# One transpose for the row of maxima, five transfers to send it, and a schedule in the source for every attention step

## The chip, the cores and the metric

The kernel runs on one core of a Trainium2 chip. The metric is device time in microseconds (us); the median of three runs of the kernel before is 1284.25 (1282.39 to 1284.72). PE is the matmul engine TensorE, PEld its weight loader, DVE is VectorE, ACT ScalarE, POOL GpSimd, and SP the engine that issues the DMA transfers. Each engine runs its own instructions strictly in program order and waits on semaphores for the others.

## What is computed

```python
q_pool = q.reshape(B, H, S // 2, 2, D).mean(axis=3)        # B=8, H=8, S=1152, D=64
scores = (1 / sqrt(D)) * q_pool @ k.transpose(0, 1, 3, 2)
attn = exp(scores - scores.max(-1, keepdims=True))
attn = attn / (attn.sum(-1, keepdims=True) + 1e-9)
x = heads_side_by_side(attn @ v)                           # (8, 576, 512)
theta = x @ w_theta
y = w_tok_r @ (x * cos(theta)) + w_tok_i @ (x * sin(theta))   # over tokens
u = x + y
out = u + maximum(u @ w_ch, 0)
```

## The kernel before

The first part does the attention of 64 heads as 32 pairs of heads, each pair on the 128 partitions as two times 64; the second part, from `theta` on, does eight batches and is not touched.

A pair goes through these steps (lines of the kernel before). **Operands:** q and k are loaded (L246, L274), q is pooled by DVE (L291, tile `qk`), both are turned by DVE in two pieces into PSUM (`pt`, L320 and L322), copied by ACT as `hi` (L348), and DVE makes the rest `lo` (L359). **Maxima:** 12 groups of two matmuls (`pm`, L374) give scores of 128 queries with 384 keys for both heads, and DVE reduces each (`mx`, L381); the last 64 queries of each head are the tail, `px` and `py` (L391, L395), reduced at L396 and L397. DVE joins the partial maxima into one column of nine per partition (`nm`, L401), turns it (`nt`, L403), and SP sends it as a row to `nmr` (L409, L410). **Scores:** 18 tiles (two halves `u` of 288 queries times nine key groups) of eight matmuls each (`pe`, L429); the last two of a tile add the row `nmr`, so a pair's first tile needs the row. ACT takes the exponential into one of 14 buffers `pc` (L432). **Sums and values:** POOL adds seven of a half's nine `pc` into `ss` (L442); PE sums the rest over keys (`pns`, L478) and multiplies all nine with `v` (`pa`, L456), 36 matmuls per half. Row sums go through memory for a reciprocal and come back as `dn` (L495 to L518); DVE scales and turns the result (L527, L532). Beside it the weights of the second part are brought to the wanted form piece by piece (L562 to L669, tiles `raw`, `wf`, `ws`, `pwt`).

All steps of a pair lie on a scale of 18 units a pair. Tables of numbers (`MAX_AT`, `PREP_AT`, `AV_AT`, `PLAN` and others) give each step's place on it, `plan` enters them for 32 pairs, and the list is emitted in the order of places. That is the order on every engine. PSUM is four slots of two banks of 512 floats. Every matmul result, small ones too, takes a whole slot; `bank2` chooses the slot at emission from three running clocks and the constants of `HOLD`. A step that is given a slot waits until the engine that read its last content is done.

Of the kernel before, what the change touches and what calls it, by code (L numbers as in the profile page):

```python
# [18 lines left out]
TAIL = 7  # L19
TAIL_LAST = 4  # L20
QP_ENG = 'vector'
DVE_SS = ()
PC_BUFS = 14
MAX_AT = (-23.312, -20.226, -18.883, -18.536, -17.347, -14.986, -12.74, -10.103, -9.854, -9.265, -8.03, -7.436)
SS_LAG = 5.804
AV_AT = (((11.793, 9),), ((17.363, 4), (18.395, 5)))
PREP_AT = {'t0': -36.588, 'hi0': -36.387, 'px': -18.64, 'lo0': -36.184, 't1': -24.925, 'hi1': -24.615, 'lo1': -24.124, 'tail': -24.631}
NS_AT = 26.57
AV_WORK = 0.49
W_FIRST = (9.45, 9.5, 9.85, 10.5, 12.75, 18.0, 18.6, 19.25, 20.45)  # L30
W_AT = (7.309, 8.637, 10.414, 10.912, 11.46, 12.125, 16.279, 17.785, 29.189, 44.405)
W_LAST = (9.4, 10.2, 11.0, 11.8, 12.6, 13.4, 14.2, 15.0, 15.8, 16.6, 17.4, 18.2, 19.0, 19.8, 20.6, 21.4, 22.2, 23.0, 23.8, 24.6)
W_END = 30
TURN_AT = 8.506
V_AT = -1.0
PRO = ({'load_k': -75.788, 'load_q': -85.873, 'pool_q': -76.236, 't0': -73.01, 'hi0': -64.408, 'lo0': -15.283, 't1': -68.701, 'hi1': -58.549, 'lo1': -53.475, 'tail': -51.925, 'px': -30.196, 'max_nm': -15.377, 'load_max': -12.729}, {'load_k': -49.139, 'load_q': -68.986, 'pool_q': -46.442, 't0': -23.223, 'hi0': -16.979, 'lo0': -10.648, 't1': -20.324, 'hi1': -14.593, 'lo1': -14.517, 'tail': -6.908, 'px': 1.104}, {'t0': 3.186, 'hi0': 3.765, 'lo0': 3.821})
MAX_AT0 = (-52.472, -50.954, -45.116, -43.942, -41.943, -40.966, -38.157, -37.18, -36.005, -27.822, -27.698, -24.494)
MAX_AT1 = (-32.274, -18.203, -18.096, -17.725, -14.587, -13.206, -13.08, -11.704, -10.826, -8.296, -8.18, -7.244)
PLAN = {'load_q': -54.267, 'load_k': -39.846, 'pool_q': -40.262, 'load_max': -3.215, 'load_v': 9.606, 'max_nm': -6.746, 'norm_spread': 33.247, 'norm_load': 35.19, 'norm_recip': 38.931, 'norm_save': 45.467, 'norm_bcast': 48.28, 'norm_out': 54.162, 'norm_turn': 56.676, 'norm_store': 62.099}
MAN = ("PE", "Activation", "DVE", "Pool", "SP")  # L40
BANKS = {}
SLOTS = 4
HOLD = {'e': (19.92, 'a', 7.517), 'pm': (8.214, 'd', 2.971), 'pt': (7.034, 'ad', 2.722), 'px': (4.719, 'd', 21.159), 'py': (6.753, 'd', 17.042), 'pa': (2.703, 'a', 2.941), 'mt': (8.515, 'a', 6.594), 'ns': (4.437, 'a', 5.407), 'pw': (4.651, 'ad', 6.171)}
# [40 lines left out]
SIN_LIM = 3.1415925  # L84


@with_exitstack
def pooled_attention_moe_kernel(
# [56 lines left out]
    clock = {"p": 0.0, "a": 0.0, "d": 0.0}  # L145
    slots = [0.0] * SLOTS

    def bank2(kind, name):
        n = min(range(SLOTS), key=lambda k: slots[k])
        work, engines, after = HOLD[kind]  # L150
        psum["slot"] = n
        clock["p"] = max(clock["p"], slots[n]) + work
        end = max([clock["p"] + 0.3] + [clock[e] for e in engines]) + after
        for e in engines:
            clock[e] = end
        slots[n] = end + 0.1
        return psum["now"][0].tile([P, 2, 512], F32, tag=f"b{n}", name=name, bufs=1)

# [44 lines left out]
    with ExitStack() as p1:  # L203
        psum["now"] = (
            p1.enter_context(tc.tile_pool(name="ps1", bufs=1, space=bass.MemoryType.PSUM)),
            BANKS,
        )
# [15 lines left out]
        nt = nrm.tile([TB, P], F32, name="nt")  # L223
# [5 lines left out]
        state = {}  # L229

        def load_q(i):
            b, hp = divmod(i, NP)
            h0 = 2 * hp
            qn = inp.tile([P, 4 * QT * D], F32, tag="qn", name=f"qn{i}")
            if i == 0:
                qv = qn[0:QP].rearrange("p (h t f d) -> p h t f d", h=2, t=QT, f=2)
# [3 lines left out]
            else:  # L240
                qn = qn[:, 0:S]
                for h in range(2):
                    qv = q[b, h0 + h].rearrange("(n i t) (e s) -> e i t n s", n=3, i=32, e=2)
                    for e in range(2):
                        a = 32 * (2 * h + e)
                        nc.sync.dma_start(  # L246
                            qn[a : a + 32].rearrange("i (t n s) -> i t n s", n=3, s=32), qv[e]
                        )
            state.setdefault(i, {})["qn"] = qn

        def keys(i):
            st = state.setdefault(i, {})
            if "kn" not in st:
                qk = inp.tile([P, QT * P + S], F32, tag="qk", name=f"qk{i}")
                st["qp"] = qk[:, 0 : QT * P if i == 0 else SQ]
                st["kn"] = qk[:, QT * P :] if i == 0 else qk[:, SQ : SQ + S]
                st["q3k"] = qk[:, 0 : SQ + 3 * P]
            return st["kn"]

        def load_k(i):  # L260
            b, hp = divmod(i, NP)
            h0 = 2 * hp
            kn = keys(i)
            for h in range(2):
                if i == 0:
                    nc.sync.dma_start(
                        kn.rearrange("p (t h d) -> p t h d", t=KT, h=2)[:, :, h, :],
                        k[b, h0 + h].rearrange("(p t) d -> p t d", t=KT),
                    )
                    continue  # L270
                kv = k[b, h0 + h].rearrange("(a i t) (e s) -> e i t a s", a=4, t=KT, e=2)
                for e in range(2):
                    a = 32 * (2 * h + e)
                    nc.sync.dma_start(  # L274
                        kn[a : a + 32].rearrange("i (t a s) -> i t a s", t=KT, a=4), kv[e]
                    )

        def pool_q(i):
# [3 lines left out]
            if i == 0:  # L282
                qv = st["qn"][0:QP].rearrange("p (h t f d) -> p h t f d", h=2, t=QT, f=2)
                ov = qp[0:QP].rearrange("p (t h d) -> p t h d", t=QT, h=2)
                for h in range(2):
                    nc.vector.tensor_tensor(
                        ov[:, :, h, :], qv[:, h, :, 0, :], qv[:, h, :, 1, :], ALU.add
                    )
            else:
                qv = st["qn"].rearrange("p (t f c) -> p t f c", t=QT, f=2)  # L290
                getattr(nc, QP_ENG).tensor_tensor(  # L291
# [3 lines left out]
        def load_v(i):  # L295
# [4 lines left out]
            state[i]["vn"] = vn  # L300

        def prep(i):
            st = state[i]
            for n in ("hi", "lo"):
                st[n] = opd.tile([P, SQ + S], F32R, tag=n, name=f"{n}{i}")
            st["nmr"] = nmrs[i % 2]

        K0 = {t: SQ * (t >= 6) + t * P for t in range(KT)}
        Q0 = 6 * P

        def prep_t(i, g):
# [27 lines left out]
        def prep_parts(i, g):  # L339
            st = state[i]  # L340
            c0, w = ((0, 3 * P), (Q0, 5 * QP))[g]
            return st["pt", g][:, :, 0:w], *(
                st[n][:, c0 : c0 + 2 * w].rearrange("p (b c) -> p b c", b=2) for n in ("hi", "lo")
            )

        def prep_hi(i, g):
            src, hi, lo = prep_parts(i, g)
            nc.scalar.copy(hi, src)  # L348

        def prep_tail(i):  # L350
            st = state[i]
            tl = st["tail"] = tails[i % 2]
            c = QP - HT
            for hs in HEADS:
                nc.scalar.copy(tl[hs, hs], st["pt", 1][hs, 1, c : c + HT])

        def prep_lo(i, g):
            src, hi, lo = prep_parts(i, g)
            nc.vector.tensor_tensor(lo, src, hi.bitcast(F32), ALU.subtract)  # L359
            if i == 0:  # L360
                slots[state[i]["slot", g]] = clock["d"] + 2.0

        HEADS = (slice(0, D), slice(D, P))

        def maxpass(i):
            st = state[i]
            hi = st["hi"]
            mx = st["mx"] = sml.tile([P, KT, 3], F32, tag="mx", name=f"mx{i}")
            W = 3 * P
            for j in range(4):  # L370
                for g in range(3):
                    pm = bank2("pm", f"pm{i}_{j}{g}")
                    for h, hs in enumerate(HEADS):
                        nc.tensor.matmul(  # L374
                            pm[:, h, 0:W],
                            hi[hs, Q0 + j * P : Q0 + (j + 1) * P],
                            hi[hs, K0[3 * g] : K0[3 * g] + W],
                            start=True,
                            stop=True,
                        )  # L380
                    nc.vector.tensor_reduce(  # L381
# [722 lines left out]
```

## Time and profile before

| | |
|---|---|
| median of three runs | 1284.25 us |
| profiled execution, first to last instruction | 1283.3 us |
| PE busy | 1239.1 us (97%) |
| DVE busy | 943.8 us (74%) |
| POOL busy | 748.1 us (58%) |
| ACT busy | 672.5 us (52%) |
| first value product of pair 0 | at 47.00 us |
| first token product of the second part | at 851.37 us |

Shares are over the whole span; the two parts have different limits. Matmuls of two heads run side by side and their bars overlap, so durations of single matmuls do not add up; the distance of two starts is what a step takes. A weight load that waits shows as idle time of PEld.

### The profile page before, as it was taken

The page shows a single profiled execution, that of the slowest core. Times are in us where ns is not written, and L with a number is a line of the kernel's source. Part 1 is how long each engine was busy: PE and PEld are TensorE (multiplying, and loading weights), DVE is VectorE, ACT ScalarE, POOL GpSimd, SP SyncE. Part 2 cuts the span into 40 slices and gives each one's busy share as a digit, 9 for nine tenths or more (in the row PEclk, how much of TensorE's full clock was granted, in tenths as well). Part 3 has the DMA queues.
Part 4 walks back from the last instruction along what each step waited for, and adds up shares of the span by engine and source line. Part 5 has one row for each costly group of instructions (what it writes and reads, how often), then busy time and mean ns, then how long its engine had stood idle before and what let it go on. Part 6 is the DMA issues. An engine that isn't in the chain of part 4 may idle for free.

```text
span 1283.3 us, 29416 instructions
## 1 busy us (share of the span) xinstructions
PE 1239.1 (97%) x11633; PEld 1004.3 (78%) x11633; DVE 943.8 (74%) x1373; ACT 672.5 (52%) x1162; POOL 748.1 (58%) x540
## 2 busy tenths in 40 slices
PE   3999999999999999999999999999999999999998
PEld 2777777767777777777777777688999999999997
DVE  6879988888888888988898897565464655637452
ACT  1566566656656665665666565464343443434430
POOL 0498768778786877778787776634323333232320
PEclk7999999999999999999999999999999999999999
DMA  5646555656656466555556542424534525244231
GB/s 92 128 83 135 116 131 111 122 118 149 119 113 133 111 139 131 120 117 130 123 124 123 119 104 60 126 93 98 103 49 84 97 32 108 39 89 97 36 47 37
DMA packets 482235, 131.05 MB, mean 102 GB/s; under 512 B 451745, under 2 KB 452129, under 8 KB 482097
## 3 DMA queue, kind: packets, MB, share of 16 engines
q1 hardware_dynamic: 481920, 128.71, 47.8%
q8 instruction: 91, 1.49, 0.5%
q0 software_dynamic: 176, 0.46, 0.1%
q14 instruction: 48, 0.39, 0.1%
HBM read 97.21 MB, written 30.70 MB: 100 GB/s over the span
## 4 chain that ended last, share of the span: by engine, by line
PE 83%; DVE 8%; issue 3%; DMA 2%; POOL 2%; ACT 1%; SPq 0%; DVEq 0%; POOLq 0%; ACTq 0%
PE pa L456 20%; PE pe L429 19%; PE py L924 17%; PE pr L963 8%; PE pth L836 8%; PE pm L374 6%; DVE mx L381 4%; PE pns L478 3%; POOL ss L442 1%; DVE qk L291 1%; PE px L391 1%; DMA nmr<-nt 1%; DVE wf L599 1%; DVE mx L396 1%; DMA rc<-rd 1%
## 5 line engine op out<-in xcount | busy, mean ns | idle before, releaser
L442 POOL TENSOR_TENSOR ss<-ss,pc 128x576 f32<-128x576 f32 x314 | 463.5, 1476 | 52.5 <-ACT pc L432 32.2
L381 DVE TENSOR_REDUCE mx<-pm 128x2 f32<-128x768 f32 x384 | 357.0, 953 | 80.0 <-PE pm L374 77.9
L432 ACT ACTIVATE pc<-pe 128x576 f32<-128x576 f32 x576 | 349.8, 652 | 75.0 <-PE pe L429 61.7
L456 PE MATMUL pa<-pc,vn 128*64 128x288 f32 x2304 | 300.4, 410 | 0.4 <-ACT pc L432 0.4
L456 PEld LDWEIGHTS pa<-pc,vn 128*64 128x64 f32 x2304 | 156.9, 137 | 108.7 <-issue 5.7
L924 PE MATMUL py<-wtk,Z 128*128 128x288 f32 x1728 | 233.8, 296 | 0.0
L924 PEld LDWEIGHTS py<-wtk,Z 128*128 128x128 f32 x1728 | 232.3, 189 | 1.3
L897 POOL TENSOR_TENSOR Z<-ab,Z 128x512 fp32r<-128x512 f32 x40 | 52.1, 1303 | 258.8 <-ACT Z L893 251.8
L429 PE MATMUL pe<-hi 64*128 64x288 f32 x1152 | 182.0, 311 | 0.3 <-DVE lo L359 0.2
L429 PE MATMUL pe<-nmr,oner 64*128 64x288 f32 x1152 | 171.2, 292 | 0.0
L429 PE MATMUL pe<-lo,hi 64*128 64x288 f32 x1152 | 170.9, 292 | 0.0
L429 PE MATMUL pe<-hi,lo 64*128 64x288 f32 x1152 | 170.7, 292 | 0.0
L442 POOL TENSOR_TENSOR ss<-pc,pc 128x576 f32<-128x576 f32 x64 | 91.9, 1435 | 126.4 <-ACT pc L432 126.0
L374 PE MATMUL pm<-hi 64*128 64x384 f32 x768 | 145.7, 377 | 16.2 <-ACT hi L348 5.8
L429 PEld LDWEIGHTS pe<-hi 64*128 64x128 f32 x1152 | 109.3, 185 | 24.2 <-issue 7.5
L374 PEld LDWEIGHTS pm<-hi 64*128 64x128 f32 x768 | 73.2, 187 | 64.0 <-DVE mx L381 16.5
L348 ACT CAST hi<-pt 128x768 fp32r<-128x768 f32 x64 | 56.3, 879 | 114.2 <-DVE pt L320 105.3
L429 PEld LDWEIGHTS pe<-lo,hi 64*128 64x128 f32 x1152 | 109.9, 186 | 0.0
L429 PEld LDWEIGHTS pe<-hi,lo 64*128 64x128 f32 x1152 | 109.6, 186 | 0.0
L429 PEld LDWEIGHTS pe<-nmr,oner 64*128 64x128 f32 x1152 | 109.1, 185 | 0.0
L963 PEld LDWEIGHTS pr<-us,wch 128*128 128x128 f32 x768 | 104.2, 189 | 1.6
L963 PE MATMUL pr<-us,wch 128*128 128x288 f32 x768 | 105.2, 296 | 0.0
(101 smaller groups left out, 1426.8 us busy)
## 6 DMA issues: line engine op xcount, KB each, us to landing
vn<-in_v_dram SPq DMA_DIRECT2D x32, 576.0 KB
qn<-in_q_dram SPq DMA_DIRECT2D x124, 144.0 KB
qk<-in_k_dram SPq DMA_DIRECT2D x124, 144.0 KB
dn<-ro SPq DMA_DIRECT2D x64, 144.0 KB
xd<-xu SPq DMA_DIRECT2D x32, 288.0 KB
xbd<-xb SPq DMA_DIRECT2D x32, 288.0 KB
xT<-xd SPq DMA_DIRECT2D x8, 1152.0 KB
xn<-xbd SPq DMA_DIRECT2D x140, 64.0 KB
```

Of the source, the lines that this page charges most:

```text
L348: nc.scalar.copy(hi, src)
L374: nc.tensor.matmul(pm[:, h, 0:W], hi[hs, Q0 + j * P : Q0 + (j + 1) * P], hi[hs, K0[3 * g] : K0[3 * g] + W], start=True, stop=True,)
L381: nc.vector.tensor_reduce(mx[:, j : j + 5 : 4, g : g + 1], pm[:, :, 0:W], AX.X, ALU.max)
L429: nc.tensor.matmul(pe[:, h, 0:HALF], w[hs], x[hs], start=(n == 0), stop=(n == 3))
L432: nc.scalar.activation(pcs[u, kt], pe[:, :, 0:HALF], AF.Exp, scale=SC)
L442: eng.tensor_tensor(st["ss", u], first, st["pc"][u, kt], ALU.add)
L456: nc.tensor.matmul(pa[hs, 0, 0:HALF], st["vn"][:, h, (kt + 3) % KT, :], st["pc"][u, kt][:, h, :], start=(kt == 0), stop=(kt == KT - 1),)
L478: nc.tensor.matmul(px[a : a + 32, 1, 0:HALF], ones, sets[u][n][:, h, :], start=(n == 0), stop=(n == len(sets[0]) - 1), tile_position=(0, a),)
L836: nc.tensor.matmul(th, xs[c][:, j * P : (j + 1) * P], ws[:, c], start=(n == 0), stop=(n == 11))
L897: engine("zlo", b).tensor_tensor(Z[1], t, Z[0].bitcast(F32), ALU.subtract)
L924: nc.tensor.matmul(st["py", c, u][:, 0:HALF], Z[zi][:, c * P : (c + 1) * P], wtk[wi][:, kw, u * HALF : (u + 1) * HALF], start=(i == 0 and ...
L963: nc.tensor.matmul(pr[u][:, 0:HALF], wch[wi][:, c, e * P : (e + 1) * P], st["us", ui][:, c, u * HALF : (u + 1) * HALF], start=(n == 0), st ...
```

## The change

Two things. First, the row of maxima: `nt` is now 128 x 32, DVE turns `nm` in one instruction, so that the nine rows of each 32 queries stand in four blocks of partitions; five transfers (four for the blocks, one for the tail) put them in place, each for both heads. Second, the tables and `plan` are gone. `operations` lists every step with its engine, the time it keeps the engine, its latency, what it depends on and how it uses PSUM; `schedule` keeps a clock per engine, the PSUM banks and the 14 buffers, and always takes the step that can begin first. In the steady pairs each engine's next step is given by `PLACE` (and one weight step beside it), so the table sets the order there; for the first two pairs and the last it may look eight steps ahead. Value products, row sums and the tail's last piece now take one bank of a slot (`acq` 2, `half`). The arithmetic is the same.

```diff
-        nt = nrm.tile([TB, P], F32, name="nt")
+        nt = nrm.tile([P, TB], F32, name="nt")
...
-            for g in range(0, P, TB):
-                nc.vector.transpose(nt[:, g : g + TB], nm[g : g + TB])
+            nc.vector.transpose(nt, nm)
...
-            for h in range(2):
-                row = nmr[h * D : h * D + 1]
-                nc.sync.dma_start(row[:, 0 : 4 * P], nt[4 * h : 4 * h + 4])
-                nc.sync.dma_start(row[:, 4 * P : SQ], nt[8:9, h * HT : (h + 1) * HT])
+            rows = nmrs[op.i % 2].bitcast(F32).rearrange("(h d) c -> h d c", h=2)[:, 0]
+            g = op.a
+            if g < 4:
+                dst = rows[:, 0 : 4 * P].rearrange("h (c g r) -> h c g r", c=4, g=4)[:, :, g]
+                src = nt[TB * g : TB * g + 8]
+            else:
+                dst = rows[:, 4 * P : SQ].rearrange("h (g r) -> h g r", g=2)
+                src = nt.rearrange("(g c) r -> g c r", g=4)[:, 8]
+            nc.sync.dma_start(dst, src)
...
-AV_AT = (((11.793, 9),), ((17.363, 4), (18.395, 5)))
...
+    "av11": 19.00002, "av12": 19.28072, "av13": 19.82686, "av14": 19.97701, "av15": 20.54731,
...
+        s["nt"] = add(DVE, 0.212, 0.22, "nt", i, "nm", 0.001, [s["nm"]] + back(i, 1, "lm"))
...
+                prev = add(PE, 0.482, 0.642, "av", i, f"av{u}", 0.01 * k, [X[u, k], s["lv"], prev or first], COL64, a=u, b=k, acq=2 * int(k == 0))
...
+    def ahead(e):
+        if e == SP:
+            return 24
+        edge = main[e] and (main[e][0].i < 2 or main[e][0].i >= NPAIRS - 1)
+        return LOOK if edge else 1
...
+        for op in schedule(operations()):
+            steps[op.name](op)
```

How the order moves is shown at two places. The first is PE in the middle of the program, from the tail maxima of one pair to the second value product of the pair before it (`pa_1` before; `b_101` to `b_104` are the four slots afterwards), with the semaphores that a row waits for. Before:

```order
L391 MATMUL px_8297<-hi_7937,tail_120 128x512 [waits DVE_49]
L391 MATMUL px_8297<-hi_7937,tail_120 128x256 x2
L395 MATMUL py_8301<-hi_7937,tail_120 128x128 [waits Activation_49]
L456 MATMUL pa_1_8305<-pc_10_8118,vn_7912 64x288 [waits Activation_49]
L456 MATMUL pa_1_8305<-pc_10_8118,vn_7912 64x288
L456 MATMUL pa_1_8305<-pc_11_8136,vn_7912 64x288 x2
L456 MATMUL pa_1_8305<-pc_12_8152,vn_7912 64x288 x2
L456 MATMUL pa_1_8305<-pc_13_8196,vn_7912 64x288 x2
L374 MATMUL pm_10_8318<-hi_7937 128x384 [waits DVE_49]
```

In the change:

```order
L784 MATMUL b_104<-hi_7162,tail_124 128x512 [waits Activation_49]
L784 MATMUL b_104<-hi_7162,tail_124 128x256 x2
L784 MATMUL b_103<-hi_7162,tail_124 128x128 [waits Activation_49]
L844 MATMUL b_103<-pc_10_7334,vn_6824 64x288 x2
L844 MATMUL b_103<-pc_11_7346,vn_6824 64x288 x2
L844 MATMUL b_103<-pc_12_7353,vn_6824 64x288 x2
L844 MATMUL b_103<-pc_13_7416,vn_6824 64x288 [waits DVE_49]
L844 MATMUL b_103<-pc_13_7416,vn_6824 64x288
L844 MATMUL b_103<-pc_14_7431,vn_6824 64x288 x2
L844 MATMUL b_103<-pc_15_7443,vn_6824 64x288 x2
L844 MATMUL b_103<-pc_16_7455,vn_6824 64x288 x2
```

The value product was left after four of its nine tiles for a pm and a score tile, and is now run through; it stands in the same slot as the tail's last piece, and its fourth tile waits for DVE. The tail's first piece waits for ACT instead of DVE.

The second place is DVE between two pairs, from the last pm reduction of one (`mx<-pm`) to the tail of the next. Before:

```order
L381 TENSOR_REDUCE mx_6289<-pm_32_6607 128x2
L322 STREAM_TRANSPOSE pt_18_6624<-qk_6305 128x2x480
L401 TENSOR_REDUCE nm<-mx_6289 128x9
L403 STREAM_TRANSPOSE nt<-nm 32x32 x4
L359 TENSOR_TENSOR lo_6394<-pt_18_6624,hi_6393 128x960
L381 TENSOR_REDUCE mx_6675<-pm_00_6676 128x2
L291 TENSOR_TENSOR qk_6691<-qn_6402 128x576
L381 TENSOR_REDUCE mx_6675<-pm_01_6725 128x2
L381 TENSOR_REDUCE mx_6675<-pm_02_6757 128x2
L396 TENSOR_REDUCE mx_6675<-px_6763 128x2
```

In the change:

```order
L770 TENSOR_REDUCE mx_6021<-b_103 128x2
L709 STREAM_TRANSPOSE b_102<-qk_5994 128x2x480
L747 TENSOR_TENSOR lo_6116<-b_102,hi_6115 128x960
L770 TENSOR_REDUCE mx_6358<-b_101 128x2
L793 TENSOR_REDUCE nm<-mx_6021 128x9
L796 STREAM_TRANSPOSE nt<-nm 128x32
L770 TENSOR_REDUCE mx_6358<-b_102 128x2
L911 TENSOR_TENSOR xu_5661<-xu_5661,dn_6263 128x576
L770 TENSOR_REDUCE mx_6358<-b_102 128x2
L790 TENSOR_REDUCE mx_6358<-b_104 128x2
```

`nm` and `nt` stand two rows later, behind `lo` and the next pair's first reduction; the pooling of q has left the place after that reduction, and the scaling of an older pair (`xu`) stands after the second.

## Rows read from the trace of the kernel before

**Rows 1.** The page's costliest groups: POOL's additions; busy us, mean ns, idle before.
```profile
L442 POOL TENSOR_TENSOR ss<-ss,pc 128x576 f32<-128x576 f32 x314 | 463.5, 1476 | 52.5 <-ACT pc L432 32.2
```
**Rows 2.** Stretches: us, busy us of PE, PEld, DVE, ACT, POOL, granted clock, DMA.
```profile
25.00:50.00 25.00, 17.02 (x150) 13.64 (x152) 23.02 (x34) 12.35 (x22) 11.33 (x8) 0.73 0.47 93
...
400.00:500.00 100.00, 98.49 (x1084) 72.12 (x1080) 88.78 (x121) 60.46 (x107) 79.19 (x57) 1.00 0.59 127
```
**Rows 3.** The chain that ended last, in time: start us, us, what.
```profile
47.00 4.52 PE pa L456 x36
...
121.80 4.52 PE pa L456 x36
...
796.47 4.52 PE pa L456 x36
...
851.37 21.59 PE py L924 x162
```
**Rows 4.** Timeline of PE within one pair: start us, us, what; idle before.
```profile
402.16 0.30 PE L429 MATMUL pe<-hi 64*128 64x288 f32 x2
...
402.69 0.29 PE L429 MATMUL pe<-hi 64*128 64x288 f32 x2
...
403.75 0.34 PE L374 MATMUL pm<-hi 64*128 64x384 f32 x2
403.93 0.30 PE L429 MATMUL pe<-hi 64*128 64x288 f32 x2
...
405.00 0.33 PE L374 MATMUL pm<-hi 64*128 64x384 f32 x2
405.94 0.74 PE L391 MATMUL px<-hi,tail 128*128 128x512 f32 x3 [0.61 <-DVE mx L381]
...
406.67 2.16 PE L456 MATMUL pa<-pc,vn 128*64 128x288 f32 x16
408.90 0.44 PE L374 MATMUL pm<-hi 64*128 64x384 f32 x2
409.18 0.31 PE L429 MATMUL pe<-hi 64*128 64x288 f32 x2
...
409.82 2.65 PE L456 MATMUL pa<-pc,vn 128*64 128x288 f32 x20
412.39 0.44 PE L374 MATMUL pm<-hi 64*128 64x384 f32 x2
...
417.79 0.69 PE L478 MATMUL pns<-ss,ones 128*32 128x288 f32 x8
...
419.38 0.44 PE L374 MATMUL pm<-hi 64*128 64x384 f32 x2
```
**Rows 5.** Groups on PEld, 121.8 to 771.7 us (26 pairs): busy, mean ns, idle before.
```profile
L429 PEld LDWEIGHTS pe<-hi 64*128 64x128 f32 x936 | 88.2, 184 | 17.8 <-DVE lo L359 5.3 <-issue 4.8 <-DVE wf L595 1.3
L374 PEld LDWEIGHTS pm<-hi 64*128 64x128 f32 x624 | 58.7, 184 | 39.8 <-DVE mx L381 10.7 <-issue 9.0 <-DVE xu L527 6.1
...
L391 PEld LDWEIGHTS px<-hi,tail 128*128 128x128 f32 x78 | 12.6, 188 | 15.8 <-DVE mx L381 14.2 <-issue 0.6
```
**Rows 6.** Groups on DVE in the same stretch.
```profile
L381 DVE TENSOR_REDUCE mx<-pm 128x2 f32<-128x768 f32 x313 | 291.6, 953 | 64.4 <-PE pm L374 62.7
...
L403 DVE STREAM_TRANSPOSE nt<-nm 32x32 f32<-32x32 f32 x104 | 20.8, 200 | 1.9
```
**Rows 7.** Timeline of SP: the row's first and last of four transfers.
```profile
426.91 0.81 SPq L409 DMA_DIRECT2D nmr<-nt  x1
...
429.12 0.52 SPq L410 DMA_DIRECT2D nmr<-nt  x1
```
**Rows 8.** Timeline of PE: the first score tile that uses this row.
```profile
433.79 0.29 PE L429 MATMUL pe<-hi 64*128 64x288 f32 x2
```
**Rows 9.** The chain within 700 to 706 us.
```profile
701.52 2.95 DMA nmr<-nt
```
**Rows 10.** Timeline of PE: the first score tile of the kernel.
```profile
33.13 0.44 PE L429 MATMUL pe<-hi 64*128 64x288 f32 x2
```

More of the change, by code (lines that the diff above doesn't have):

```diff
@@ L84, with __init__ @@
 SIN_LIM = 3.1415925
+class Op:
+    def __init__(self, eng, busy, lat, name, i, a, b, place, off, deps, mode, acq):
+        self.eng, self.busy, self.lat, self.name = eng, busy, lat, name
+        self.i, self.a, self.b, self.place, self.off = i, a, b, place, off
+        self.deps = [d for d in deps if d is not None]
+        self.mode, self.acq, self.owner, self.last, self.ends = mode, acq, None, False, 0
+        self.takes, self.readers, self.reads, self.two = False, 0, [], False
+        self.slot = None
@@ L143, in bank @@
         return pool.tile([P, 512], F32, tag=kind, name=name, bufs=bufs[kind])
[L145 to L157, printed above, removed]
     def segments(j):
@@ L203, in pooled_attention_moe_kernel @@
     with ExitStack() as p1:
[L204 to L207, printed above, removed]
+        ps1 = p1.enter_context(tc.tile_pool(name="ps1", bufs=1, space=bass.MemoryType.PSUM))
+        slots = [ps1.tile([P, 2, 512], F32, name=f"b{n}") for n in range(SLOTS)]
         inp = p1.enter_context(tc.tile_pool(name="inp", bufs=1))
@@ L363, in pooled_attention_moe_kernel @@
[L363 to L381, printed above, removed]
-                        mx[:, j : j + 5 : 4, g : g + 1], pm[:, :, 0:W], AX.X, ALU.max
-                    )
-                    yield
@@ new lines, in prep_lo, with maxima, max_mm @@
+        def prep_lo(op):
+            src, hi, lo = prep_parts(op.i, op.a)
+            nc.vector.tensor_tensor(lo, src, hi.bitcast(F32), ALU.subtract)
+        def maxima(i):
+            st = state[i]
+            if "mx" not in st:
+                st["mx"] = sml.tile([P, KT, 3], F32, tag="mx", name=f"mx{i}")
+            return st["mx"]
+        def max_mm(op):
+            hi, j, g = state[op.i]["hi"], op.a, op.b
+            q = Q0 + j * P
+            pm = slots[op.slot]
+            for h, hs in enumerate(HEADS):
+                nc.tensor.matmul(
+                    pm[:, h, 0:W],
+                    hi[hs, q : q + P],
+                    hi[hs, group(g)],
+                    start=True,
+                    stop=True,
+                )
@@ new lines, in max_red, with half, tail_mm @@
+        def max_red(op):
+            j, g = op.a, op.b
+            nc.vector.tensor_reduce(
+                maxima(op.i)[:, j : j + 5 : 4, g : g + 1], slots[op.slot][:, :, 0:W], AX.X, ALU.max
+            )
+        def half(op):
+            return slots[op.slot // 2][:, op.slot % 2]
+        def tail_mm(op):
+            st = state[op.i]
+            if op.a == 0:
+                parts = [(slots[op.slot][:, n, c : c + w], k) for n, c, k, w in TAIL_KEYS]
+            else:
+                parts = [(half(op)[:, 0:P], Q0 + SQ + 2 * P)]
+            for out, k in parts:
+                nc.tensor.matmul(
+                    out, st["tail"], st["hi"][:, k : k + out.shape[1]], start=True, stop=True
+                )
@@ new lines, in escore, with expo, ssum @@
+                        start=bool(op.acq and n == 0), stop=(n == len(terms) - 1),
+                        skip_group_check=not op.acq,
+                    )
+        def expo(op):
+            u, k = op.a, op.b
+            pc = pch.tile([P, 2, HALF], F32, tag="pc", name=f"pc{op.i}_{u}{k}")
+            state[op.i].setdefault("pc", {})[u, k] = pc
+            nc.scalar.activation(pc, slots[op.slot][:, :, 0:HALF], AF.Exp, scale=SC)
+        def ssum(op):
+            st, u, k = state[op.i], op.a, op.b
+            if k == 1:
+                st["ss", u] = nrm.tile([P, 2, HALF], F32, tag=f"ss{u}", name=f"ss{u}_{op.i}", bufs=2)
+            first = st["pc"][u, 0] if k == 1 else st["ss", u]
+            nc.gpsimd.tensor_tensor(st["ss", u], first, st["pc"][u, k], ALU.add)
@@ new lines, in av, with av_out @@
+        def av(op):
+            st, u, k = state[op.i], op.a, op.b
+            for h, hs in enumerate(HEADS):
+                nc.tensor.matmul(
+                    half(op)[hs, 0:HALF],
+                    st["vn"][:, h, key(u, k), :],
+                    st["pc"][u, k][:, h, :],
+                    start=(k == 0),
+                    stop=(k == KT - 1),
+                )
+        def av_out(op):
+            st, u = state[op.i], op.a
+            if "xu" not in st:
+                st["xu"] = nrm.tile([P, 2, HALF], F32, tag="xu", name=f"xu{op.i}", bufs=3)
+            nc.scalar.copy(st["xu"][:, u, :], half(op)[:, 0:HALF])
@@ new lines, in norm_sum @@
+        def norm_sum(op):
+            st, n = state[op.i], op.a
+            tail = TAIL if op.i < NPAIR - 1 else TAIL_LAST
+            for h in range(2):
+                for u in range(2):
+                    a = 32 * (2 * h + u)
+                    src = st["ss", u] if n == 0 else st["pc"][u, tail + n - 1]
+                    nc.tensor.matmul(
+                        half(op)[a : a + 32, 0:HALF],
+                        ones,
+                        src[:, h, :],
+                        start=(n == 0),
+                        stop=(n == KT - tail),
+                        tile_position=(0, a),
+                    )
@@ new lines, in w_sums, with w_fetch @@
+        def w_sums(jb):
+            if "ws" not in jb:
+                jb["ws"] = wst.tile([P, SQ], F32, tag="ws", name="ws")
+            return jb["ws"], three(jb["ws"][0 : jb["R"], 0 : 3 * -(-jb["cols"] // 3)])
+        def w_fetch(op):
+            jb = job(op)
+            n = jb["cols"]
+            for dst, src in jb["parts"]:
+                nc.sync.dma_start(jb["raw"][dst, 0:n], src)
+            if jb["more"] is not None:
+                nc.sync.dma_start(jb["raw"][:, n : n + 1], jb["more"])
```

949 lines of the change are left out of this document (555 added, 394 removed), and 64 rows, old and new, of the table PLACE.

## The prediction

> **What bounds the kernel now.** I read first the table of stretches [rows 2]. Between 400 and 500 us TensorE (PE) is busy 98.49 of 100 us at full clock, VectorE (DVE) 88.78, GpSimd (POOL) 79.19. The reader is to see that PE is the bound and that two engines behind it have little room. Then the chain that ended last [rows 3]: the first half's value product of a pair begins at 47.00 (pair 0), 121.80 (pair 3) and 796.47 (pair 30), so a pair takes (796.47 - 47.00) / 30 = 24.98 us. The second half of the program starts its token products at 851.37; its code is not touched, so what it takes is kept.
>
> A PE that is "98% busy" need not be at work: matmul bars overlap, so a wait of 0.1 us leaves no idle record. So I price the work of one pair by starts in one pair's timeline [rows 4]. A score tile is 402.69 - 402.16 = 0.53; a maximum group (pm) 403.93 - 403.75 = 0.18; an unbroken value product of nine tiles 4.52 [rows 3]; the three tail maxima with their exit 406.67 - 405.94 = 0.73; the row sums 419.38 - 417.79 = 1.59. The sum for a pair: 18 x 0.53 + 12 x 0.18 + 2 x 4.52 + 0.73 + 1.59 = 23.06. To it I add 0.28 for entering another array shape (about 0.1 each before the first value product, the tail and the sums: a pm that follows another shape takes 409.18 - 408.90 = 0.28 instead of 0.18) and 0.2 as an allowance for weight turns, which only some pairs have: 23.54. The pair takes 24.98, so 1.44 us in each are no work. One part is the second value product, cut in two around a pm and a score tile: its pieces take 408.90 - 406.67 = 2.23 and 412.39 - 409.82 = 2.57, 0.28 more than 4.52; some 0.2 of it is the second change of shape (one exit and one entry at about 0.1). The other 1.25 are waits. Where they are is seen at the weight loader [rows 5]: in 26 pairs it idled 15.8 us before tail maxima, 39.8 before pm and 17.8 before a tile's first term, mostly released by DVE. Each of these needs one of four PSUM slots that a DVE reduction of 0.953 us [rows 6] or an exponential must leave first. One is open to view: the tail, 405.00 + 0.18 + 0.09 = 405.27 at best, starts at 405.94 after 0.61 idle.
>
> **The change part by part.** *Turn.* Four 32x32 transposes become one of 128x32. Four took 4 x 0.20 = 0.80 us a pair [rows 6]. The new form is in no row: at least one old one, 0.20, at most all four, 0.80. I take 0.2, the nearest row being one instruction on the same 32 columns. That saves DVE 0.6 us a pair; it lies beside PE's work, so alone it is worth nothing to the span, but it shortens the way to the row of maxima.
>
> *Row.* Four transfers become five. The issues stand (429.12 - 426.91) / 3 = 0.74 apart [rows 7], so five take 3.7 and the last is issued 0.74 later. SP issues in order; behind them stand the next pair's loads of v and q, which have many microseconds. In the old order the last issue at 429.12 plus the landing of 2.95 that the chain shows [rows 9] is 432.07, 1.7 before the first score tile of the pair at 433.79 [rows 8]. That chain row also says that in some pairs the row already comes too late. In the new order the transpose stands one pm reduction behind the next pair's first pm. From that pm PE still has 6 score tiles, 4 pm, the tail and an unbroken value product: 3.2 + 0.7 + 0.7 + 4.5 = 9.1. DVE uses 0.95 + 0.15 + 0.2 = 1.3 of it, the five issues 3.7, a landing 2.95: 7.95, so 1.1 us are left. It is hidden, with less cover than before.
>
> [...]
>
> *Order, steady pairs.* The second value product is no longer cut: minus 0.2. The tail's last piece, the value products and the row sums now take one bank, not a two-bank slot, and the slot of every step is fixed by a schedule that carries all five engines, where the old code guessed it from three clocks. On DVE the pooling of q has left the first pm reductions of a pair, but the scaling of `xu` has come between the second and the third, nearer to the tail; the tail's first piece now waits for ACT to have left a slot, not for a pm reduction. The bounds: all 1.25 us of waits stay (24.98 - 0.2 = 24.8 a pair), or none (23.54). The rows do not show the new order, so I choose: I let a third stay, 0.45, since a pm still holds a slot for 0.34 + 0.95 and 12 of them share four slots with 18 tiles. A pair then takes 24.0, minus 1.0, and 30 steady pairs minus 30 us (bounds minus 6 and minus 43).
>
> One new tie costs. The order with its waits shows that the second value product now shares a slot with the tail's last piece, and its fourth tile waits for DVE to have reduced that piece. PE gets there 0.15 + 3 x 0.5 = 1.65 after the tail's first piece (0.15 of the 0.73 being its last piece); DVE reduces 1152 elements a row there, by an estimate from a pm's 768 [rows 6] in 0.953 x 1152 / 768 = 1.43: 0.2 to spare, if DVE comes at once. The tie is paid from the 0.45.
>
> *Start.* The first score tile is at 33.13 [rows 10], the first value product at 47.00 [rows 3]: 13.9 us. Now only 12 tiles and two pm stand between: 6.7 us at full clock. [...] I take 3.5, bounds 0 and 4.5.
>
> *End.* After the last full pair both orders hold the same score tiles, two value products and 24 sums, and the products' start at 851.37 keeps its distance from the value product at 796.47 [rows 3]: 0, within 1. The sums of pair 30 now stand behind all twelve tiles instead of nine, 1.6 us later; their norm reaches DVE shortly before PE ends its own 15 us, so I cost it at nothing.
>
> **Sum.** 1283.3 of the profiled span - 30 - 3.5 = 1249.8. The median of the runs, 1284.25, is 0.95 above that span: 1250.8, put down as 1250.
>
> **The rivals.** (a) *Waits move rather than go.* PE faster by 4% leaves DVE less room: 88.78 busy of 100 over pairs 4% shorter would be 92, less the 0.6 saved about 90. Where DVE is late by one weight step, the fourth tile of the value product and the slots behind it wait as the tail did. If 0.95 of the 1.25 stay, a pair is 24.5: minus 14, start nothing: 1270. For it: DVE is named in nearly all the waits. Against: the wait at the tail, the one stop in open view, no longer hangs on DVE.
>
> (b) *Nearly all waits go.* 23.6 a pair, 1.38 x 30 = 41, start and end 4.5: 1239. For it: DVE and POOL together have room. Against: twelve slots held 1.3 us each.
>
> (c) *The row of maxima comes late: slower.* If a landing takes twice 2.95, 5.9, the first tile of every pair stands 5.9 - 4.0 = 1.9 behind the end of the value product, with all PE behind it: 24.0 + 1.9 = 25.9, plus 0.9 x 30 = 27, minus 3.5: 1308. It decides from a landing of about 5.0 (as much as is gained). [...] Against: each of the five carries 1 KB or less.
>
> (d) *Exponentials wait for buffers: slower.* There are 14. Before the row sums of a pair, nine tiles of the next are out, and four of the old are kept for the sums; one is left for additions that POOL owes. The new POOL row puts the first half's last additions behind four or five of the second half. One addition late, 1.476 [rows 1], is 24.0 + 1.48 = 25.5 a pair: 1284.25 + 15 - 3.5 = 1296. Against: POOL has 20 us free in 100.
>
> (e) *Nothing happens*: gains and the ties cancel, 1284.
>
> **How the numbers follow.** Forecast 0.50, (a) 0.20, (b) 0.13, (c) 0.07, (d) 0.05, (e) 0.05. I keep 0.83 for faster by over 0.2%, about what a measurement of this kernel tells from none, 0.05 for within it, 0.12 for slower. The range 1236 to 1274 reaches from (b) past (a); it leaves out (c), (d), (e) and the edges. The likeliest case by itself is 1244 to 1258.
>
> **What would show it.** In the profile after: the distance of the first value products of two pairs 24.0 (23.6 to 24.4 bears the forecast out, 24.5 and more is (a)); the second value product as one piece of 36 matmuls of about 4.5; the weight loader's idle time before tail and pm down to about a third; one transpose of about 0.2 a pair. Wrong would be: a stop of PE at the first tile's fourth term released by the row's transfer (c), exponentials released by POOL (d), a first value product at 47 or later, or token products that start less than 14 us before 851.37.

## The result, and the profile after

The changed kernel takes 1296.56 us (median of 4 runs, 1295.37 to 1297.29) against 1284.49 (4 runs): ratio 1.0097, interval 1.0083 to 1.0111. It is slower by 1%, where 2.7% faster was forecast. The time lies outside the range and on the other side.

The stretch that [rows 2] shows of before, after (columns as there): TensorE (PE) is less busy, VectorE (DVE) hardly freer.

```profile
400.00:500.00 100.00, 97.58 (x1069) 71.60 (x1065) 87.17 (x109) 59.91 (x108) 75.82 (x53) 1.00 0.58 126
```

PE's timeline (start us, us, what, idle before and its releaser) at the first score tile (with the tail of pair 1 ahead of it), the first value product of pair 0 and of pair 30, and the first token product:

```profile
36.80 1.22 PE L784 MATMUL b<-hi,tail 128*128 128x512 f32 x3 [0.18 <-DVE lo L747]
37.96 0.61 PE L822 MATMUL b<-hi 64*128 64x288 f32 x2
...
46.76 0.71 PE L844 MATMUL b<-pc,vn 128*64 128x288 f32 x4
...
807.65 0.71 PE L844 MATMUL b<-pc,vn 128*64 128x288 f32 x4
...
862.88 0.56 PE L1263 MATMUL py<-wtk,Z 128*128 128x288 f32 x3
```

Read the same way, before has 46.93 and 796.39, each 0.07 to 0.08 ahead of the chain's piece [rows 3]. A pair takes (807.65 - 46.76) / 30 = 25.36 us instead of 24.98: 30 x 0.38 = 11.4 us lost, 3.2 of them in the first two pairs (27.39 and 25.89 us against 24.94 and 25.13). The rest nearly cancels (span 1293.5 - 1283.3 = 10.2).

Where it stops is one place, in every pair up to pair 29. PE and DVE around the tail of one pair, after:

```profile
412.03 1.02 PE L784 MATMUL b<-hi,tail 128*128 128x512 f32 x4
412.98 1.68 PE L844 MATMUL b<-pc,vn 128*64 128x288 f32 x12
415.11 1.19 PE L844 MATMUL b<-pc,vn 128*64 128x288 f32 x8 [0.46 <-DVE mx L790]
```
```profile
410.48 1.87 DVE L911 TENSOR_TENSOR xu<-xu,dn 128x576 f32<-128x576 f32 x1
412.27 0.95 DVE L770 TENSOR_REDUCE mx<-b 128x2 f32<-128x768 f32 x1
413.14 1.21 DVE L790 TENSOR_REDUCE mx<-b 128x2 f32<-128x1024 f32 x1
414.77 0.29 DVE L790 TENSOR_REDUCE mx<-b 128x1 f32<-128x128 f32 x1 [0.42 <-PE b L844]
```

The second value product (L844) stops after three tiles (x12) until DVE has reduced the tail's last piece, and DVE idles before that reduction *until PE has ended the third tile*. Each waits for the other. In the program's order the reduction stands between the third and the fourth tile, and both use halves of one PSUM tile, so it waits for the third tile and the fourth waits for it. Within the product the matmuls' starts stand, two by two, 0.24 apart; here it is 0.87: 0.63 us lost. Where a weight turn stands between the tail and the product (nine times), the same stop comes behind the first tile.

The weight loader's idle time, after, 124.8 to 781.5 us (26 pairs; [rows 5] shows before):

```profile
L844 PEld LDWEIGHTS b<-pc,vn 128*64 128x64 f32 x1872 | 127.4, 137 | 111.5 <-DVE mx L790 25.2 <-ACT pc L832 6.5 <-issue 1.5
L822 PEld LDWEIGHTS b<-hi 64*128 64x128 f32 x936 | 88.0, 184 | 7.2 <-DVE mx L770 3.0
L760 PEld LDWEIGHTS b<-hi 64*128 64x128 f32 x624 | 55.6, 183 | 35.0 <-issue 31.7 <-DVE lo L747 1.8 <-ACT wf L990 1.4
L784 PEld LDWEIGHTS b<-hi,tail 128*128 128x128 f32 x104 | 17.4, 187 | 11.7 <-ACT pc L832 9.6 <-DVE mx L770 0.9
```

DVE no longer holds up the tail or pm; 25.2 us of waits for its reduction L790 have come to the value product (111.5 us of idle time, 88.5 before in as many pairs). Before pm the idle time has hardly fallen, 35.0 after 39.8, and is now put down to no engine. On DVE itself (busy us, mean ns), for [rows 6]:

```profile
L770 DVE TENSOR_REDUCE mx<-b 128x2 f32<-128x768 f32 x313 | 291.5, 946 | 50.7 <-PE b L760 49.0
L911 DVE TENSOR_TENSOR xu<-xu,dn 128x576 f32<-128x576 f32 x26 | 48.1, 1851 | 0.0
...
L796 DVE STREAM_TRANSPOSE nt<-nm 128x32 f32<-128x32 f32 x26 | 5.5, 211 | 0.9
```

The one transpose takes 0.211, as estimated. But the scaling of `xu` takes 1851 ns, and took 844 on the mean in the kernel before:

```profile
L527 DVE TENSOR_TENSOR xu<-xu,dn 128x576 f32<-128x576 f32 x26 | 21.9, 844 | 0.0
```

### The profile page after: what moved, and what is told of

The parts are those of the page before. It is cut to its first block, busy times and chain, and to the rows that moved or that the text cites. A ratio compares the mean times of both kernels' runs of the same rounds, so it can differ in the third digit from the quotient of the medians.

```text
span 1293.5 us, 29498 instructions
## 1 busy us (share of the span) xinstructions
PE 1241.4 (96%) x11633; PEld 1002.9 (78%) x11633; DVE 938.0 (73%) x1277; ACT 663.3 (51%) x1162; POOL 743.3 (57%) x540
## 3 DMA queue, kind: packets, MB, share of 16 engines
q8 instruction: 91, 1.49, 0.5%
## 4 chain that ended last, share of the span: by engine, by line
PE 78%; DVE 9%; DMA 4%; ACT 3%; issue 3%; SPq 2%; POOL 1%; DVEq 0%; POOLq 0%; ACTq 0%
PE b L822 19%; PE b L844 17%; PE py L1263 16%; PE pth L1175 7%; PE pr L1302 7%; PE b L760 5%; PE b L865 4%; DVE mx L770 3%; DMA qk<-in_k_dram 2%; PE b L784 2%; DVE xu L911 1%; ACT pc L832 1%; DVE b L709 1%; DVE mx L790 1%; DVE lo L747 1%
## 5 line engine op out<-in xcount | busy, mean ns | idle before, releaser
L770 DVE TENSOR_REDUCE mx<-b 128x2 f32<-128x768 f32 x384 | 356.9, 946 | 64.1 <-PE b L760 60.5
L832 ACT ACTIVATE pc<-b 128x576 f32<-128x576 f32 x576 | 339.3, 654 | 58.7 <-PE b L822 37.3
L844 PE MATMUL b<-pc,vn 128*64 128x288 f32 x2304 | 300.6, 410 | 14.9 <-DVE mx L790 13.8
L844 PEld LDWEIGHTS b<-pc,vn 128*64 128x64 f32 x2304 | 156.9, 137 | 137.6 <-DVE mx L790 29.0
L822 PE MATMUL b<-hi 64*128 64x288 f32 x1152 | 178.1, 305 | 1.3 <-ACT xu L856 0.6
L822 PE MATMUL b<-lo,hi 64*128 64x288 f32 x1152 | 170.8, 292 | 0.0
L822 PE MATMUL b<-hi,lo 64*128 64x288 f32 x1152 | 170.5, 292 | 0.0
L822 PE MATMUL b<-nmr,oner 64*128 64x288 f32 x1152 | 170.2, 291 | 0.0
L760 PE MATMUL b<-hi 64*128 64x384 f32 x768 | 134.5, 374 | 11.6 <-ACT hi L736 4.8
L822 PEld LDWEIGHTS b<-hi 64*128 64x128 f32 x1152 | 108.8, 185 | 12.5 <-DVE mx L770 4.3
L760 PEld LDWEIGHTS b<-hi 64*128 64x128 f32 x768 | 70.1, 188 | 57.9 <-issue 36.4
```

Of the source, the lines that this page charges most:

```text
L760: nc.tensor.matmul(pm[:, h, 0:W], hi[hs, q : q + P], hi[hs, group(g)], start=True, stop=True,)
L770: nc.vector.tensor_reduce(maxima(op.i)[:, j : j + 5 : 4, g : g + 1], slots[op.slot][:, :, 0:W], AX.X, ALU.max)
L822: nc.tensor.matmul(pe[:, h, 0:HALF], w[hs], x[hs], start=bool(op.acq and n == 0), stop=(n == len(terms) - 1), skip_group_check=not op.acq,)
L832: nc.scalar.activation(pc, slots[op.slot][:, :, 0:HALF], AF.Exp, scale=SC)
L844: nc.tensor.matmul(half(op)[hs, 0:HALF], st["vn"][:, h, key(u, k), :], st["pc"][u, k][:, h, :], start=(k == 0), stop=(k == KT - 1),)
```

## The experiments

All times are medians; ratios are to the kernel before on the same chip. Theory A: the tie is the loss, and the waits that I wanted to remove were mostly none.

**Undo the tie.** In the schedule's search for a slot:

```
                 t, slot = pair_slot() if op.acq == 1 else one_slot(at)
+                if op.name == "av" and op.a == 1:
+                    t, slot = pair_slot()
+                    slot = 2 * slot
```

> The changed kernel, with one rule added to its schedule: the second value product takes a PSUM slot that the tail's last piece does not share. Theory A (the tie between the second value product and the reduction of the tail's last piece is the loss): the stop of 0.63 us between the third and the fourth tile of that product goes in every pair, a pair without a weight turn takes 24.2 instead of 24.82 us, and 30 pairs give back 19 us: 1296.6 - 19 = 1278, 1274 to 1282. Rival B (VectorE has no room, so the stop only moves to another slot): 24.6 to 24.9 a pair, 1290 to 1297.

1288.74, ratio 1.0036 (1.0024 to 1.0048): 8 us back, not 19, so neither theory's number. The product is whole again, but now waits before its first tile for the pm reduction that DVE does after the scaling:

```profile
410.42 0.95 PE L847 MATMUL b<-pc,vn 128*64 128x288 f32 x6 [0.27 <-DVE mx L773]
```

A pair without a weight turn takes 24.42 (24.82 with the tie), one with a turn mostly 25.69 or 26.28, on the mean no less than with the tie (25.89 and 25.87).

**Keep the tie, reduce first.** For each pair `px` piece 1 and its reduction are moved ahead of piece 0 in the emitted order.

> The changed kernel with its tie kept, but the tail's last piece comes before the other three, and its reduction stands before theirs on VectorE; the second value product's first tile then waits for that reduction, not its fourth. Theory A (the price of the tie is how late VectorE comes to that reduction): one pm reduction of 0.95 and the piece's own 0.29 stand before it, so PE stops for about 0.45 instead of 0.63 us: 5 us less, 1291, 1286 to 1295. If only the place of the reduction between the third and fourth tile counted, the stop would be gone: 1278. Rival B: 1296, nothing.

1289.04, ratio 1.0045 (1.0032 to 1.0058), in A's range, but not by A's mechanism: in most pairs PE now stops 0.70 us before the tail, for a slot that an exponential still holds. The wait has moved from one user of the slots to another.

**The turn and the row alone, and the order alone.**

```
-            for g in range(0, P, TB):
-                nc.vector.transpose(nt[:, g : g + TB], nm[g : g + TB])
+            nc.vector.transpose(nt, nm)
...
+            for g in range(4):
+                nc.sync.dma_start(part[:, :, g], nt[TB * g : TB * g + 8])
+            nc.sync.dma_start(last, nt.rearrange("(g c) r -> g c r", g=4)[:, 8])
```

> The kernel before with only the turn and the row changed: one transpose of 128x32 instead of four of 32x32, five transfers instead of four; the order of the instructions as before. Theory A: the row is hidden and VectorE has room, 1284.5, within 2 us. Rival C (the row's five transfers with small pieces are the loss): at least 4 us more, up to the 12 us of the whole change, 1288 to 1297.

1284.63, ratio 1.0001 (0.9993 to 1.001): no cost and no gain. The reverse edit in the changed kernel:

> The changed kernel with the old turn and row: four transposes of 32x32 and four transfers, the new order kept. Theory A: the order alone makes the kernel slower, 1296.6, within 3 us (0.6 us more on VectorE in a pair can cost a little). Rival C (the row is the loss): 1284 to 1292.

1303.06, ratio 1.0146 (1.0131 to 1.016): 6.5 us more than the change, so both theories missed it. The row is innocent: by old_row5 its new form costs nothing, and going back to the old one gains nothing. In the new order the 0.6 us that DVE takes longer in a pair are worth 0.2 us of PE's. In the pairs without a turn 4, 7 and 9 all of it lies at one pm: it starts 0.1 late, 0.05 us after the reduction behind the four transposes has ended, and the tile behind it another 0.1 late. The rest does not come through, since the scaling that follows takes 1.20 instead of 1.85 us on the mean; why is shown below.

**Take away the late reductions.** `pm[:, :, 0:W]` becomes `pm[:, :, 0:48]` in the reduction of the kernel before, and in the two new orders likewise; these kernels leave out most keys when they take the maxima.

> The kernel before, order unchanged, with the twelve pm reductions of a pair over 2 x 48 columns instead of 2 x 384, so VectorE leaves each slot at once; the maxima are then taken over part of the keys. It shows what the waits for these slots cost. The forecast's account (1.25 us of waits in a pair): a pair goes from 24.98 to about 23.75. Theory A (only starts far above the constant distances of a transition are waits: 0.51 in a pair; the rest of the 1.25 are fixed costs after a change of array shape): 24.5 a pair, 15 us less, and a start shortened by some 5 us: 1262 to 1270. By the forecast's account 1240 to 1248.

1260.60, ratio 0.9821.

> The changed kernel with the same short pm reductions (2 x 48 columns; maxima over part of the keys), tie kept. Theory A: the tie does not hang on VectorE's load, since VectorE waits there for PE's third tile: the stop of 0.63 stays in every pair, pairs without a turn take 24.7 to 24.8. Rival B (VectorE is late at the tie): the stop shrinks to under 0.2 and pairs take 24.2. The total by A 1270 to 1288 (start and turn pairs shortened too).

1277.31, ratio 0.9949.

> own_slot with the same short pm reductions (maxima over part of the keys): the new order with neither the tie nor late reductions. Theory A: 24.1 a pair without a turn, so 18 us less than new_short_max (30 x 0.6), and only 0.3 to 0.4 a pair less than the kernel before with short reductions: the new order by itself has little to give. The forecast's account: 23.5 a pair.

1263.87, ratio 0.9843. Starts of the first value products, from PE's timelines:

| kernel | pair 0, us | pair 30, us | mean of 30 | pair without a turn |
|---|---|---|---|---|
| before | 46.93 | 796.39 | 24.98 | 24.3 to 25.2 |
| old_short_max | 40.98 | 772.65 | 24.39 | 24.15 |
| after | 46.76 | 807.65 | 25.36 | 24.82 |
| own_slot | 46.66 | 800.16 | 25.12 | 24.42 |
| new_short_max | 42.00 | 789.05 | 24.90 | 24.62 |
| own_short_max | 43.43 | 775.52 | 24.40 | 23.94 |

Late reductions cost the old order 24.98 - 24.39 = 0.59 us a pair, not 1.25. The weight loader's idle time, on which the forecast read the waits off, hardly falls with them (113 to 770 us, 27 pairs; 39.8 in [rows 5]):

```profile
L374 PEld LDWEIGHTS pm<-hi 64*128 64x128 f32 x642 | 60.7, 184 | 35.7 <-issue 31.8 <-DVE xu L527 3.5 <-DVE pt L320 0.4
```

The tie stays when DVE is idle, as A said (new_short_max, PE and DVE):

```profile
401.26 1.68 PE L844 MATMUL b<-pc,vn 128*64 128x288 f32 x12
403.40 3.13 PE L844 MATMUL b<-pc,vn 128*64 128x288 f32 x24 [0.46 <-DVE mx L790]
```
```profile
403.05 0.29 DVE L790 TENSOR_REDUCE mx<-b 128x1 f32<-128x128 f32 x1 [0.68 <-PE b L844]
```

It costs 24.62 - 23.94 = 0.68 in a pair without a turn and 24.90 - 24.40 = 0.50 on the mean. With the full reductions it costs half of that, 25.36 - 25.12 = 0.24 (own_slot): late reductions then stop PE just ahead of the same product. Without tie and late reductions the two orders take the same: 24.39 and 24.40.

**The turns.** own_slot with a rule that lets a turn stand only ahead of the row sums:

```
+            if op.name == "w_turn" and main[e] and (main[e][0].name, main[e][0].a) != ("ns", 0):
+                at = far
```

> The kernel own_slot with one more rule: a weight turn (five transposes on PE) may stand only ahead of the row sums, where the kernel before has it, and no longer right behind the tail. Theory A2 (own_slot fell short by its ten pairs with a turn: they take 25.69 or 26.28 us where the others take 24.42, since the turn asks for a PSUM slot just when all four are held): a turn costs 0.64 us as in the kernel before, such pairs take 25.1, 10 x 0.9 = 9 us less than own_slot: 1280, 1277 to 1283, and faster than the kernel before (1284.6). Rival B2 (the turn only shows a lack of slots that then stops another step): 1286 to 1290.

1293.31, ratio 1.0064 (1.005 to 1.0078): slower. Yet pair 28 begins its product at 743.70 instead of 749.25; the loss comes later, where PE waits for the second half's first load; the last turn now stands at 830.9 instead of 784.6. From the view of waits, 805 to 862 us (us in total, times, longest):

```profile
PE pxn L1160 <- DMA xT<-xd: 6.5, 1, 6.5
```

With the rule only up to pair 28 (`main[e][0].i < 28 and`):

> own_turn, but its rule on the weight turns ends with pair 28. In own_turn the last turn waited for the row sums of pair 30 (830.9 us instead of 784.6), and the second half's first loads with it (PE stood 6.5 us for them). Theory A2: the pairs up to the 28th are those of own_turn (value product of pair 28 at 743.7), the rest that of own_slot (538.0 us from there): 1281.7 of span, 1283 in the runs, 1280 to 1286. If the turns were not what own_slot lost by: 1288 to 1292.

1283.68, ratio 0.9997 (0.9988 to 1.0006), as A2 said (own_slot fell short by its pairs with a turn); the place of the turns was 5 us.

**The old order with the product in one piece.** `AV_AT[1]` is `((17.363, 9),)` and then `((18.395, 9),)` instead of `((17.363, 4), (18.395, 5))`.

> The kernel before with one edit: the second value product stands in one piece right behind the tail, and the pm and the score tile that cut it come after it (as the changed kernel has it); all else, turn and row too, as before. The forecast's term for this, two changes of array shape less, is 0.2 us a pair: 6 us less, 1278.5, 1276 to 1281. Rival B (VectorE's reductions come no earlier, so the waits grow by what the product gives): 1283 to 1288.

> The kernel before with the second value product in one piece at its later place: tail, then the pm and the score tile, then all nine tiles. One change of array shape less than before, two slots more asked for while the tail holds two. If only the shapes counted: 0.1 to 0.15 us a pair, 4 us less, 1280.5. Theory A (the slots are short at the tail, a wait appears there): the pm or the tile behind the tail waits up to 0.7 us a pair: 1290 to 1305.

1358.62, ratio 1.0583 (1.0568 to 1.0597), and 1342.04, ratio 1.0452 (1.0438 to 1.0466). Nothing expected of the first held, and of the second only that slots are short at the tail, at three times the price. PE and DVE of the first, behind the product:

```profile
417.75 0.34 PE L374 MATMUL pm<-hi 64*128 64x384 f32 x2
419.31 0.48 PE L429 MATMUL pe<-hi 64*128 64x288 f32 x2 [1.22 <-DVE lo L359]
```
```profile
417.43 0.96 DVE L381 TENSOR_REDUCE mx<-pm 128x2 f32<-128x768 f32 x1 [3.20 <-PE pm L374]
418.30 0.95 DVE L359 TENSOR_TENSOR lo<-pt,hi 128x768 fp32r<-128x768 f32 x1
```

The pm that cut the product fed DVE. Put behind it, it leaves DVE idle for 3.20 us with `lo` queued behind its reduction, and the next tile waits for `lo`: 24 such waits, 33.7 us together, from 113 to 770 us (some 25 pairs), about half of what a pair has lost (27.51 instead of 24.98). The cut was not a cost but a cover.

**Why own_slot's product waits.** DVE and POOL of own_turn28 ahead of a tail:

```profile
404.23 1.86 DVE L916 TENSOR_TENSOR xu<-xu,dn 128x576 f32<-128x576 f32 x1
```
```profile
402.66 2.82 POOL L844 TENSOR_TENSOR ss<-ss,pc 128x576 f32<-128x576 f32 x2
...
405.55 1.83 POOL L844 TENSOR_TENSOR ss<-ss,pc 128x576 f32<-128x576 f32 x1
```

The scaling ends 0.6 after POOL's addition in flight does at 402.66 + 2.82 = 405.48, and POOL's next addition takes 1.83 instead of 1.41. This is so every time. In the traces of before, after, own_slot and own_turn28, 99 scalings begin while a POOL instruction is in flight, and all end 0.61 or 0.62 us after it has ended; 25 begin with none in flight or about to start, and take 0.73 to 0.76. POOL's addition behind such a scaling takes 1.80 to 1.94. So each holds the other up here: the scaling by 1.1 us (1.86 against 0.75), the addition behind it by 0.4 (1.83 against 1.41). The schedule already adds what is left of POOL's addition to this step (`op.two`); it places the step there all the same. So the 844 ns of the kernel before are a mixture: nine of its 32 scalings meet POOL, in the new order 31.

```
-            nc.vector.tensor_tensor(st["xu"], st["xu"], st["dn"], ALU.mult)
+            nc.vector.tensor_scalar(st["xu"], st["xu"], st["dn"][:, 0, 0:1], None, op0=ALU.mult)
```

> own_turn28 with the scaling of xu by one column of dn (an instruction with one tensor operand, no second tensor read) at the same place on VectorE: the normaliser is then not the right one for every column. Theory D (the scaling waits on VectorE for a GpSimd addition to end, 1.86 instead of 0.84 us, and the pm reduction behind it frees its slot 1 us late): the scaling takes 0.75, the second value product starts without a wait, a pair without a turn takes 24.1 instead of 24.43: 10 us less, 1273.5, 1270 to 1277. Rival (the scaling takes long because of its operands or place, not GpSimd): 0.75 too, and no rival in time; if the wait is the exponential's slot instead: the wait stays at 0.2 to 0.3, 1281 to 1284.

1276.52, ratio 0.9938 (0.9926 to 0.9951). This kernel scales all columns by the normaliser of one and leaves out the others, so its time alone counts. The time is that of D (the scaling waits for POOL) and the wait at the product is gone (24.22 a pair), but the instruction still takes twice what was expected; the row of own_turn28 stands above that of own_scale1:

```profile
L916 DVE TENSOR_TENSOR xu<-xu,dn 128x576 f32<-128x576 f32 x27 | 48.1, 1781 | 0.0
```
```profile
L916 DVE TENSOR_SCALAR xu<-xu,dn 128x576 f32<-128x576 f32 x27 | 40.1, 1485 | 0.0
```

So one tensor operand does not free it: 30 of its 32 scalings meet a POOL instruction and end 0.32 after it. 1.78 - 1.49 = 0.30 us less of DVE ahead of the tail give 7 us. The scaling on GpSimd (`add(POOL, ...)`, `nc.gpsimd.tensor_tensor`, placed at 62):

> own_turn28 with the scaling of xu moved from VectorE to GpSimd, among its additions of the next pairs. The output is complete. Theory D: VectorE is 1.86 us freer in a pair and the wait at the second value product goes, GpSimd gets 1.4 us more (about 82 of 100 busy): 24.1 to 24.2 a pair, 8 us less than own_turn28: 1276, 1272 to 1280, faster than the kernel before (1284). Rival: GpSimd's additions come late for the row sums and the exponentials' buffers, 1284 to 1300.

1281.98, ratio 0.9983 (0.9974 to 0.9992). This version leaves nothing out. It is faster than the kernel before by 0.17% and than the changed one by 1.1%, less than D's range; the wait at the product is gone in 20 of the 27 pairs from 2 to 28, and now and then a score tile stops (0.56 us for a pm reduction in one pair). What keeps it behind own_scale1 was not tested.

## Why the prediction was wrong

The forecast made a pair of 24.00 us: 23.55 of work and 0.45 of waits that stay. Measured, by the table: 24.40 of work (own_short_max) and 0.96 of late reductions and tie. The two overlap, so their shares depend on which is taken away first: 0.46 and 0.50 with the reductions shortened first (25.36 - 24.90, 24.90 - 24.40), 0.72 and 0.24 with the tie undone first (25.12 - 24.40, 25.36 - 25.12).

- **"The other 1.25 are waits"** is the step that failed first: 0.85 x 30 = 25.5 us. I took as a wait whatever a sum of shortest distances left over. In old_short_max, where no reduction is late, most of the surcharges are still there: behind the first pm after a change of array shape the tile starts 0.28 and not 0.175 later, and once in most such runs two terms stand 0.24 apart and not 0.13. In 27 pairs (113 to 770 us) there are 80 of the first and 56 of the second, (80 x 0.105 + 56 x 0.11) / 27 = 0.54 us a pair. 26 more tiles start 0.1 late without such a change, each 0.05 us after an exponential that held their slot: 0.10 a pair that are waits, but not for DVE. With the 0.59 these make 1.23 of the 1.25. The forecast counted what it costs to enter another shape, three times, and, but for the cut product, left out what it costs to come back from it; its own row, 0.28 instead of 0.18, is of the second kind. The weight loader's idle time was no measure of waits either: before pm it stays at 35.7 us without late reductions. PE rows of old_short_max:

```profile
410.98 0.40 PE L429 MATMUL pe<-hi 64*128 64x288 f32 x2
411.22 0.29 PE L429 MATMUL pe<-lo,hi 64*128 64x288 f32 x2
411.35 0.30 PE L429 MATMUL pe<-hi,lo 64*128 64x288 f32 x2
...
414.63 0.33 PE L374 MATMUL pm<-hi 64*128 64x384 f32 x2
414.90 0.73 PE L391 MATMUL px<-hi,tail 128*128 128x512 f32 x3
```

  The distance of the first two rows, 0.24, is such a surcharge; the tail, 0.27 behind its pm, no longer waits where [rows 4] has 0.61 idle.
- **"0.2 to spare" at the new tie**: the tie was seen and mis-sized. I counted when DVE *could* reduce the piece. That the fourth tile and not the first waits for the reduction also says that the reduction was emitted between the third and the fourth, and so waits for the third: DVE idles 0.42 there. 0.24 to 0.50 a pair, 7 to 15 us. Rival (a) had the place, not the mechanism or the sign.
- **"I let a third stay, 0.45"**: 0.46 to 0.72 stayed, by the two ways above. That 0.45 is near the first is luck: it was a third of 1.25, and only 0.59 was there to begin with, so the new order gained 0.13 at most.
- **"Minus 0.2" for the uncut product**: 24.15 - 23.94 = 0.21 without a turn, right in the new order. Ten turns at 25.13 - 23.94 = 1.19 instead of 24.85 - 24.15 = 0.70 (the same two runs), and a first pair of 26.08 instead of 24.16, eat it: about (10 x 0.49 + 1.92) / 30 = 0.23. The forecast called the turns "0.2 as an allowance" and did not ask where they went.
- **Start, "I take 3.5"**: 0.2 came. No run shows the 3.5 that the sum takes for it. From first tile to product it is 46.76 - 37.96 = 8.8 us, 2.1 more than the 6.7 of twelve tiles and two pm: the first three tiles take 41.01 - 37.96 = 3.05 instead of 3 x 0.53 = 1.59, their terms 0.24 apart and not 0.13, though the trace has the granted clock at 1.00 from 37.96 to 41.00 (before, from 33.13 to 38.12 they stand 0.24 apart too, at a clock of 0.50). Still it is 5.1 less than the 13.9 of before, but the first tile comes at 37.96 instead of 33.13 [rows 10]. The forecast counted what no longer stands between tile and product and did not ask where it had gone. Before, nine pm and the tail of pair 1 stand between them; after, two pm. Three of the pm and that tail now stand ahead of the first tile (18 pm and two tails, before 15 and one), and PE goes through them at DVE's pace (idle 0.18 to 0.34 us before each of the last four, 34.20 to 36.80); the first tile follows that tail without a wait (36.80 and 37.96 above). So the row of maxima, which DVE closes at 31.35 (L793) instead of 27.44 (L401), is not what the tile waits for, and the last issue 0.74 later, which the forecast counted, does not bear on it. How much each of the moved steps costs was not tested; with short reductions the first tile still comes 6.1 us later than in the old order (33.23 and 27.09, new_short_max and old_short_max).
- **Turn and row**: "alone it is worth nothing" and "hidden" hold (old_row5). Rivals (c) and (d) did not come. The 4.0 of (c) is the landing of 2.95 and the 1.1 us that were left; the row's pieces of 32 floats, 128 B, where it had 128, 512 B, cost nothing measurable (1.0001, old_row5). That the 0.6 us of DVE are worth 6.5 us in the new order was not foreseen.

Sum of the misses: 3.3 at the start, 30 x 1.36 = 41 in the pairs, less 1.1 at the end (1293.5 - 807.65 against 1283.3 - 796.39) is 43, but for rounding the 1293.5 - 1249.8 = 43.7 of the spans.

## What to carry to other kernels

A residual is not a wait: before you price one, look whether the same distance also appears where nothing is late, or shorten the suspected work and see what stays. When two engines work in one buffer tile, read the waits in both directions; a reader emitted between two writers tied them both here (after, at one tail: VectorE idle 0.42 us, PE 0.46), even though they use different halves. Before you count a step as gone from one place, find where it now stands. A piece that cuts a long product may be what feeds the engine behind it. When you take two causes away, do it in both orders before you share the loss out between them.

## What was not expected of the hardware

The granted clock of PE fell after short stops: in the old order with the product in one piece, PE idled 0.50 us until 416.95 and 1.22 until 419.31, and the next 3.7 us ran at 0.54 (columns as in [rows 2]):

```profile
417.00:419.30 2.30, 1.09 (x12) 0.81 (x12) 1.87 (x3) 1.25 (x2) 0.00 (x0) 1.00 0.52 82
419.30:423.00 3.70, 3.69 (x32) 3.69 (x34) 2.48 (x5) 1.78 (x3) 1.59 (x2) 0.54 0.40 151
```

Terms then start 0.24 instead of 0.13 apart (419.58, 419.82, 420.06; 417.23, 417.36, 417.49 ahead of the stop): of the 3.7 us some 1.7 are lost (an estimate from the 0.54), more than the second stop itself. And the same scaling on DVE takes 0.75 us or up to 1.96 (817.75, after), by how much of a POOL addition is still in flight when it begins, which no count of instructions shows.
